# The first activations of a fused convolution and gated feed-forward kernel: loaded as fp32 in four pieces by SyncE and ScalarE, cast by ScalarE

## The chip, the cores and the metric

The kernel runs on one core of a Trainium2 chip. The metric is the device time of one execution in microseconds, as the median of several runs. Five engines of the core take part: TensorE (PE), VectorE (DVE), ScalarE (ACT), GpSimd (POOL) and SyncE (SP). SP, ScalarE and GpSimd can issue DMA transfers; a transfer that also converts fp32 to fp16 on its way is issued by GpSimd in this kernel.

## The reference

There are two steps. A lightweight causal convolution over `x` (8 x 4096 x 192, fp32): each of 8 heads covers 24 of the 192 channels and has 7 taps, which are a softmax over `weight` (8 x 7). Then a gated feed-forward of width 1536 over all 32768 tokens:

```python
w = softmax(weight)                                   # per head, 7 taps
conv[b, s, h, :] = sum_k w[h, k] * x_pad[b, s + k, h, :]   # 6 zeros ahead of each sequence
t = conv.reshape(32768, 192)
out = (np.maximum(t @ w_gate, 0) * (t @ w_val)) @ w_out    # 192 -> 1536 -> 192
```

## The kernel before

The eight sequences are handled as two streams (`st` 0 and 1: sequence b and b + 4) of which 1024 tokens each make a unit; there are 16 units (`NUNIT`). A unit's convolved activations lie transposed in `xc[u]` (64 channels of each of the two streams on 128 partitions, three channel blocks `c`, 1024 tokens). `gate_val` multiplies them with `Wg` and `Wv` (line 505, matmuls 512 wide), ScalarE applies the ReLU (line 516), VectorE multiplies (line 517), and `project` multiplies with `Wo` (lines 536, 556, 594). The convolution of units 2 to 15 is done with per-channel multiplications on VectorE, ScalarE and GpSimd beside the matmuls of earlier units; units 0 and 1 are convolved on TensorE with band matrices.

The order of work on each engine is the order of the program (`manual_schedule`); waits come from the data. The start, which the change touches, goes as follows.

- **The first x.** The first window is 512 tokens of both streams, in `xts[0]`, cut into five blocks `jj` of 104 tokens with 6 tokens of history. Blocks 1 to 4 of stream 0 are loaded by SP as fp32 (line 125) into a staging place in the room of the tile `prods`, which is not needed until later, and are cast by ScalarE in one instruction (line 279). Blocks 1 to 4 of stream 1 are loaded by GpSimd straight into fp16 (line 130). Block 0 of both streams is loaded by SP as fp32 (line 141) behind rows that VectorE has set to zero (line 140) and cast by VectorE (line 294).
- **The taps and the bands.** SP loads `weight` (line 104); VectorE takes the maximum (line 214), ScalarE the exponential (line 217), ahead of which its table load (line 148) and a first, unused exponential stand; VectorE the sum, its reciprocal and the scaled head selection `over` (lines 221 to 224). GpSimd makes a mask (`affine_select`, line 131) for it. TensorE spreads the taps (lines 235 and 255) into two PSUM tiles, and these are copied into band matrices: heads 0 to 2 and head 3 by VectorE, heads 4 to 7 by ScalarE (line 288, `fill_band`). Short matmuls on constants (line 157, `warm_up`) stand in TensorE's gaps.
- **The first window.** `conv_dense(0, c)` for `c` = 0, 1, 2 multiplies the blocks with the bands (line 333). For `c` = 0 the order is blocks 1 to 4 of stream 0, blocks 1 to 4 of stream 1, then block 0 of both. Channel block 0 takes heads 0 to 2, block 1 heads 2 to 5, block 2 heads 5 to 7. ScalarE copies channel blocks 0 and 2 to `xc[0]`, VectorE block 1 (line 343). Then the first `gate_val` begins.
- **Weights.** GpSimd loads `Wg` and `Wv` in six cuts of columns with a cast (line 173, `load_w`) to partitions 0 to 63. The other 64 partitions are copied on the core: cuts 0 and 1 by VectorE (`both_halves`), the others by GpSimd (`pool_halves`, line 180). Between the weights GpSimd loads the second window's x (`load_x(1)`, line 90), and after them what the later units need.

Of the kernel before, what the change touches and what calls it, by code (L numbers as in the profile page):

```python
# [9 lines left out]
F16 = mybir.dt.float16  # L10
# [5 lines left out]
def kernel(  # L16
# [12 lines left out]
    nc = tc.nc  # L29

    B, S, D = x.shape
    H, KW = weight.shape
    G = D // H
    DFF = moe_w_gate.shape[1]
    PAD = KW - 1
    NB = B // 2
    NCH = D // 64
    NBLK = D // 32
    NFF = DFF // 128
    WIN = 512  # L40
    NWIN = S // WIN
    SUB = 112
# [4 lines left out]
    GSUB = 5  # L47
    DSUB = 104
# [13 lines left out]
    const = ctx.enter_context(tc.tile_pool(name="const", bufs=1))  # L62
# [35 lines left out]
    xts = {}  # L98
    ROWS0 = DSUB + PAD
# [7 lines left out]
    def stage(p0, rows, st, n_st, jj, n):  # L107
        at = room[p0 : p0 + rows, 0, 0, 0:1]
        dims = [[D * GSUB, n_st], [D, n], [1, D]]
        return bass.AP(  # L110
            tensor=at.tensor,
            offset=at.offset + D * (GSUB * st + jj),
            ap=[at.ap[0]] + [d for d in dims if d[1] > 1],
        )

    xts[0] = xpool.tile([128, GSUB, 2, D], F16, name="x_h")

    def body(st):
        return bass.AP(
            tensor=x.tensor,  # L120
            offset=x.offset + (NB * st * S + DSUB - PAD) * D,
            ap=[[D, SUB], [DSUB * D, GSUB - 1], [1, D]],
        )

    nc.sync.dma_start(out=stage(0, SUB, 0, 1, 1, GSUB - 1), in_=body(0))
    ones = const.tile([128, SUB], FP)
    nc.vector.memset(ones[:], 1.0)
    spaced = const.tile([SUB, KW, SEG + 2 * GAP], FP)
    nc.gpsimd.memset(spaced[:], 0.0)  # L129
    nc.gpsimd.dma_start(out=xts[0][0:SUB, 1:GSUB, 1, :], in_=body(1))  # L130
    nc.gpsimd.affine_select(
        out=spaced[:, :, GAP : GAP + SEG],
        in_=ones[0:SUB, 0 : KW * SEG].rearrange("p (k s) -> p k s", k=KW),
# [8 lines left out]
        out=stage(PAD, DSUB, 0, 2, 0, 1),  # L142
        in_=bass.AP(
            tensor=x.tensor, offset=x.offset, ap=[[D, DSUB], [NB * S * D, 2], [1, D]]
        ),
    )
    spare = const.tile([H, 1], FP)
    nc.scalar.activation(spare[:], ones[0:H, 0:1], ACTF.Exp)

# [12 lines left out]

    Wg = const.tile([128, NCH, DFF], F16)
    Wv = const.tile([128, NCH, DFF], F16)
    Wo = const.tile([128, NFF, D], F16)
    CUTS = [0, 128, 384, 640, 896, 1152, DFF]

    def load_w(s, to=None):  # L170
        cols = slice(CUTS[s], CUTS[to or s + 1])
        for src, dst in ((moe_w_gate, Wg), (moe_w_val, Wv)):
            nc.gpsimd.dma_start(
                out=dst[0:64, :, cols],
                in_=src.rearrange("(c p) f -> p c f", p=64)[:, :, cols],
            )

    def both_halves(copy, s, dst):
        cols = slice(CUTS[s], CUTS[s + 1])
        copy(out=dst[64:128, :, cols], in_=dst[0:64, :, cols])  # L180

    def pool_halves(s):
        both_halves(nc.gpsimd.tensor_copy, s, Wg)
        both_halves(nc.gpsimd.tensor_copy, s, Wv)

    load_w(0)
    load_w(1)
    load_w(2)
    xts[1] = load_x(1)
    load_w(3)  # L190
    pool_halves(2)
    load_w(4, 6)
    pool_halves(3)

    ex = const.tile([H, KW + 1, SEG], FP)
# [3 lines left out]
    def summed(out, step, n, at):  # L199
# [15 lines left out]
        out=mx[:], in_=wr[:], axis=mybir.AxisListType.X, op=ALU.max, negate=True  # L215
# [9 lines left out]
        out=over[:],  # L225
# [10 lines left out]
        out=spread[0:SUB, 0, 0:H],  # L236
# [7 lines left out]
    with nc.allow_low_precision("products with one and zero"):  # L244
        nc.vector.tensor_tensor(
            out=diag[:],
# [6 lines left out]
    for a in range(2):  # L253
        for b in range(NSEG):
            nc.tensor.matmul(
                out=(bps, spread)[a][:, a, HB * SEG * b : HB * SEG * (b + 1)],
# [12 lines left out]
    for h in range(H):  # L269
        r = G * h  # L270
        while r < G * (h + 1):
            c, n = r // 64, min(64 - r % 64, G * (h + 1) - r)
            nc.sync.dma_start(
                out=tap[r % 64 : r % 64 + n, c, :],
                in_=taps[h : h + 1, :].unsqueeze(1).to_broadcast([1, n, KW]),
            )
            r += n

    nc.scalar.copy(out=xts[0][0:ROWS0, 1:GSUB, 0, :], in_=stage(0, ROWS0, 0, 1, 1, GSUB - 1))
    bands = {}  # L280

    def fill_band(a, heads, copy):
        lo, n = heads[0] - HB * a, len(heads)
        part = const.tile([128, n, SUB], F16, name=f"band{heads[0]}")
        for i, h in enumerate(heads):
            bands[h] = part[0 : SUB + PAD, i, :]
        from_ = (bps, spread)[a][:, a, 0 : HB * SUB]
        copy(
            out=part[:].rearrange("p h (b s) -> p h b s", s=SEG),
            in_=from_.rearrange("p (b h s) -> p h b s", h=HB, s=SEG)[:, lo : lo + n],  # L290
        )

    fill_band(0, [0, 1, 2], nc.vector.tensor_copy)
    nc.vector.tensor_copy(out=xts[0][0:ROWS0, 0, :, :], in_=stage(0, ROWS0, 0, 2, 0, 1))
    fill_band(0, [3], nc.vector.tensor_copy)
    fill_band(1, [4, 5, 6, 7], nc.scalar.copy)

# [10 lines left out]
    def conv_dense(g, c):  # L308
# [3 lines left out]
        if g == 0 and c == 0:  # L312
            xc[0] = xcpool.tile([128, NCH, UNIT], F16, name="xc")
            both_halves(nc.vector.tensor_copy, 0, Wg)
            both_halves(nc.vector.tensor_copy, 0, Wv)
# [324 lines left out]
    both_halves(nc.vector.tensor_copy, 1, Wg)  # L640
    both_halves(nc.vector.tensor_copy, 1, Wv)
    pool_halves(4)
    pool_halves(5)
    nc.gpsimd.tensor_copy(out=tap[64:128], in_=tap[0:64])
# [71 lines left out]
```

## Time and profile before

| | |
|---|---|
| Median of 3 runs | 767.79 us (767.7 to 768.71) |
| Profiled execution, its own time | 767.88 us |
| Span in its profile | 765.9 us |
| TensorE busy | 761.7 us (99%) |
| VectorE, ScalarE, GpSimd busy | 692.7, 600.7, 369.9 us |
| First matmul of line 505 | 7.80 us after the start of the span |

Times in the views are microseconds from the start of the span unless marked ns. A line of the timeline gives start, duration, engine, line of the kernel, operation, the tiles written and read with their shapes, and in brackets the engine's idle time just before with what ended it. In the chain of work that ended last, each piece is what the next one waited for. In the DMA view, q1 is SP's queue and q0 GpSimd's, with packets, megabytes written and the time of the packets as a share of the 16 DMA engines; it can be above 100%, since packets overlap on an engine. TensorE's matmuls are pipelined, so its busy share is not a share of its peak.

### The profile page before, as it was taken

How to read it: one execution, taken by the hardware profiler on the slowest of the kernel's cores; microseconds unless marked ns; L12 is line 12 of the kernel's file. 1: busy time of each engine (PE TensorE's matmuls, PEld its weight loads, DVE VectorE, ACT ScalarE, POOL GpSimd, SP SyncE). 2: the span in 40 equal slices, each digit the busy share in tenths (PEclk: the TensorE clock that was granted, in tenths of full speed). 3: DMA queues.
4: the chain of work that ended last, by engine and by line, in shares of the span. 5: the costliest groups of instructions: out<-in, count | busy, mean ns of one | idle time of the engine just before them, and what ended most of it. 6: DMA issues, size and time to landing. Idle time of an engine off the chain costs nothing.

```text
span 765.9 us, 24782 instructions
## 1 busy us (share of the span) xinstructions
PE 761.7 (99%) x10794; PEld 502.5 (66%) x10794; DVE 692.7 (90%) x746; ACT 600.7 (78%) x735; POOL 369.9 (48%) x212
## 2 busy tenths in 40 slices
PE   9999999999999999999999999999999999999998
PEld 4595674946749476584755848567484674947648
DVE  7999999999999999999999999999999999996591
ACT  6797887878878787887878878788787887875571
POOL 8608648093570926619166290743908346090000
PEclk9999999999999999999999999999999999999999
DMA  8966727190472804528054281722919131200202
GB/s 121 134 104 116 92 91 88 54 122 6 100 78 66 110 23 97 61 85 95 23 111 47 85 92 44 106 31 85 93 44 117 21 92 39 65 22 15 71 2 84
DMA packets 131810, 56.12 MB, mean 73 GB/s; under 512 B 96741, under 2 KB 131701, under 8 KB 131701
## 3 DMA queue, kind: packets, MB, share of 16 engines
q1 hardware_dynamic: 90789, 38.85, 25.1%
q0 software_dynamic: 40768, 15.59, 18.9%
q8 instruction: 84, 1.38, 0.8%
q14 instruction: 25, 0.20, 0.1%
q10 hardware_dynamic: 144, 0.10, 0.0%
HBM read 31.68 MB, written 25.17 MB: 74 GB/s over the span
## 4 chain that ended last, share of the span: by engine, by line
PE 99%; DMA 1%; issue 0%; POOL 0%; ACT 0%; POOLq 0%
PE ps L505 65%; PE ps L536 31%; PE ps L556 2%; DMA x_h<-in_x_dram 1%; PE ps L594 1%; PE ps L333 0%; PE ps L358 0%; POOL spaced L129 0%; ACT acc L573 0%; POOLq L700 0%
## 5 line engine op out<-in xcount | busy, mean ns | idle before, releaser
L517 DVE TENSOR_TENSOR hT<-gr,ps 128x1024 f16<-128x1024 f16 (+1 forms) x386 | 468.9, 1215 | 37.0 <-ACT gr L516 9.9
L516 ACT ACTIVATE gr<-ps 128x1024 f16<-128x1024 f32 (+1 forms) x386 | 392.9, 1019 | 102.4 <-PE ps L505 100.6
L458 POOL TENSOR_TENSOR prods<-prods 128x1344 f32<-128x1344 f32 x70 | 212.4, 3034 | 309.1 <-DVE prods L454 305.7
L505 PE MATMUL ps<-xc,Wg 64*128 64x512 f16 x2304 | 311.9, 376 | 0.0
L505 PE MATMUL ps<-xc,Wv 64*128 64x512 f16 x2304 | 311.8, 376 | 0.0
L536 PEld LDWEIGHTS <-hT 64*128 64x128 f16 x5664 | 234.1, 94 | 3.6
L536 PE MATMUL ps<-Wo,hT 64*128 64x192 f16 x5664 | 236.1, 243 | 0.0
L505 PEld LDWEIGHTS <-Wv 64*128 64x128 f16 x2304 | 129.8, 94 | 118.5 <-DVE hT L517 0.3
L505 PEld LDWEIGHTS <-Wg 64*128 64x128 f16 x2304 | 112.2, 94 | 132.4 <-issue 0.2
L481 DVE SCALAR_TENSOR_TENSOR acc<-x_r,tap,acc 128x576 f32<-128x576 f16 x210 | 154.3, 811 | 1.6 <-ACT acc L469 1.6
L452 ACT ACTIVATE prods<-x_r,tap 128x448 f32<-128x448 f16 x222 | 130.3, 662 | 0.0
L573 ACT COPY out_s<-ps 128x768 f32<-128x768 f32 (+1 forms) x63 | 45.7, 725 | 52.4 <-PE ps L536 42.5
L414 POOL DMA_DIRECT2D x_e<-in_x_dram x56 | 45.1, 818 | 3.4 <-POOL x_p L433 3.4
L433 POOL COPY x_p<-x_e 128x1728 f16<-128x1728 f16 x28 | 44.7, 1624 | 1.7 <-DMA x_e<-in_x_dram 1.6
L458 POOL TENSOR_TENSOR xc<-prods 128x1344 f16<-128x1344 f32 x14 | 42.4, 3027 | 1.1
L481 DVE SCALAR_TENSOR_TENSOR xc<-x_r,tap,acc 128x576 f16<-128x576 f16 x42 | 31.8, 810 | 0.0
L573 DVE COPY out_s<-ps 128x384 f32<-128x384 f32 x15 | 8.3, 550 | 25.5 <-ACT out_s L573 25.5
L469 ACT ACTIVATE acc<-x_r,tap 128x576 f32<-128x576 f16 x42 | 29.4, 766 | 0.0
L454 DVE TENSOR_SCALAR prods<-x_r,tap 128x448 f32<-128x448 f16 x72 | 27.3, 446 | 0.0
L556 PE MATMUL ps<-Wo,hT 128*128 128x192 f16 x192 | 16.2, 246 | 0.0
L556 PEld LDWEIGHTS <-hT 128*128 128x128 f16 x192 | 15.9, 98 | 0.0
L90 POOL DMA_DIRECT2D x_h<-in_x_dram x6 | 4.9, 825 | 0.0
(54 smaller groups left out, 66.9 us busy)
## 6 DMA issues: line engine op xcount, KB each, us to landing
out_dram<-out_s SPq DMA_DIRECT2D x63, 384.0 KB
x_e<-in_x_dram POOLq DMA_DIRECT2D x34, 192.0 KB, 6.2
x_e<-in_x_dram POOLq DMA_DIRECT2D x22, 240.0 KB, 4.8
x_r<-x_p SPq DMA_TRANSPOSE x126
Wo<-in_moe_w_out_dram POOLq DMA_DIRECT2D x1, 576.0 KB
x_h<-in_x_dram POOLq DMA_DIRECT2D x2, 240.0 KB, 7.6
x_h<-in_x_dram POOLq DMA_DIRECT2D x2, 210.0 KB, 5.1
x_h<-in_x_dram POOLq DMA_DIRECT2D x2, 192.0 KB, 7.6
```

The source lines that it names most:

```text
L414: nc.gpsimd.dma_start(out=xe[:, j : j + n, st, :, :].rearrange("p j c r -> p j (c r)"), in_=bass.AP(tensor=x.tensor, offset=x.offset + (b ...
L433: nc.gpsimd.tensor_copy(out=xp[:, :, :, st, :], in_=xe[:, :, st, :, :])
L452: engine.activation(out=out, in_=in_, func=ACTF.Copy, scale=scale)
L458: nc.gpsimd.tensor_tensor(out=pr[:, 0] if k < KW - 1 else xc[u][:, :, LDVE:UNIT], in0=pr[:, 0], in1=pr[:, k], op=ALU.add,)
L469: nc.scalar.activation(out=accs[u][:, c, :], in_=shifted(u, c, 0, 0), func=ACTF.Copy, scale=tap[:, c, 0:1],)
L481: nc.vector.scalar_tensor_tensor(out=xc[u][:, c, 0:LDVE] if k == KW - 1 else acc[:, c, :], in0=shifted(u, c, k, 0), scalar=tap[:, c, k : k ...
L505: nc.tensor.matmul(out=pss[i][:, st, :], lhsT=W[64 * st : 64 * st + 64, c, 128 * f : 128 * (f + 1)], rhs=xcb[64 * st : 64 * st + 64, c, WI ...
L516: nc.scalar.activation(out=gr[:, sts], in_=pss[0][:, sts], func=ACTF.Relu)
L517: nc.vector.tensor_tensor(out=h[:, f, sts], in0=gr[:, sts], in1=pss[1][:, sts], op=ALU.mult)
L536: mm = nc.tensor.matmul(out=outs[q], lhsT=h[64 * r : 64 * r + 64, f, st, 128 * q : 128 * (q + 1)], rhs=Wo[64 * r : 64 * r + 64, f, :], sta ...
L556: nc.tensor.matmul(out=outs[q], lhsT=h[:, f, st, 128 * q : 128 * (q + 1)], rhs=Wo[:, f, :], start=(f == 0), stop=(f == NFF - 1),)
L573: one(out=dst[:, step * j : step * j + step], in_=src[:, step * j : step * j + step])
```

## The change

All of the first x now comes as fp32 through the staging place. Blocks 1 and 2 of stream 0 are issued by ScalarE as its first instruction, blocks 3 and 4 by SP, then block 0 of both streams as before, then blocks 1 and 2 and blocks 3 and 4 of stream 1, also by SP. ScalarE casts these four pieces, each 384 columns wide, in that order, ahead of its band of heads 4 to 7. GpSimd no longer loads the first x: its first transfer is the first cut of `Wg`, ahead of the mask; the first cut of `Wv` and the rest follow as before. On VectorE the cast of block 0 goes ahead of the bands of heads 0 to 2 instead of behind them. The definitions of the weight tiles and helpers move up; only `load_w` gets a new argument.

```diff
-    def body(st):
+    def body(st, jj, n):
         return bass.AP(
             tensor=x.tensor,
-            offset=x.offset + (NB * st * S + DSUB - PAD) * D,
-            ap=[[D, SUB], [DSUB * D, GSUB - 1], [1, D]],
+            offset=x.offset + (NB * st * S + DSUB * jj - PAD) * D,
+            ap=[[D, SUB], [DSUB * D, n], [1, D]],
         )
 
-    nc.sync.dma_start(out=stage(0, SUB, 0, 1, 1, GSUB - 1), in_=body(0))
+    nc.scalar.dma_start(out=stage(0, SUB, 0, 1, 1, 2), in_=body(0, 1, 2))
+    nc.sync.dma_start(out=stage(0, SUB, 0, 1, 3, 2), in_=body(0, 3, 2))
     ones = const.tile([128, SUB], FP)
     nc.vector.memset(ones[:], 1.0)
     spaced = const.tile([SUB, KW, SEG + 2 * GAP], FP)
     nc.gpsimd.memset(spaced[:], 0.0)
-    nc.gpsimd.dma_start(out=xts[0][0:SUB, 1:GSUB, 1, :], in_=body(1))
...
+    def load_w(s, to=None, which=(0, 1)):
+        cols = slice(CUTS[s], CUTS[to or s + 1])
+        for src, dst in [((moe_w_gate, Wg), (moe_w_val, Wv))[i] for i in which]:
...
+    load_w(0, 1, (0,))
     nc.gpsimd.affine_select(
...
             tensor=x.tensor, offset=x.offset, ap=[[D, DSUB], [NB * S * D, 2], [1, D]]
         ),
     )
+    for jj in (1, 3):
+        nc.sync.dma_start(out=stage(0, SUB, 1, 1, jj, 2), in_=body(1, jj, 2))
     spare = const.tile([H, 1], FP)
     nc.scalar.activation(spare[:], ones[0:H, 0:1], ACTF.Exp)
...
-    load_w(0)
+    load_w(0, 1, (1,))
     load_w(1)
     load_w(2)
     xts[1] = load_x(1)
...
-    nc.scalar.copy(out=xts[0][0:ROWS0, 1:GSUB, 0, :], in_=stage(0, ROWS0, 0, 1, 1, GSUB - 1))
+    for st in range(2):
+        for jj in (1, 3):
+            nc.scalar.copy(
+                out=xts[0][0:ROWS0, jj : jj + 2, st, :], in_=stage(0, ROWS0, st, 1, jj, 2)
+            )
...
+    nc.vector.tensor_copy(out=xts[0][0:ROWS0, 0, :, :], in_=stage(0, ROWS0, 0, 2, 0, 1))
     fill_band(0, [0, 1, 2], nc.vector.tensor_copy)
-    nc.vector.tensor_copy(out=xts[0][0:ROWS0, 0, :, :], in_=stage(0, ROWS0, 0, 2, 0, 1))
     fill_band(0, [3], nc.vector.tensor_copy)
     fill_band(1, [4, 5, 6, 7], nc.scalar.copy)
```

More of the change, by code (lines that the diff above doesn't have):

```diff
@@ L129, with both_halves, pool_halves @@
     nc.gpsimd.memset(spaced[:], 0.0)
-    nc.gpsimd.dma_start(out=xts[0][0:SUB, 1:GSUB, 1, :], in_=body(1))
+    Wg = const.tile([128, NCH, DFF], F16)
+    Wv = const.tile([128, NCH, DFF], F16)
+    Wo = const.tile([128, NFF, D], F16)
+    CUTS = [0, 128, 384, 640, 896, 1152, DFF]
+    def load_w(s, to=None, which=(0, 1)):
+        cols = slice(CUTS[s], CUTS[to or s + 1])
+        for src, dst in [((moe_w_gate, Wg), (moe_w_val, Wv))[i] for i in which]:
+            nc.gpsimd.dma_start(
+                out=dst[0:64, :, cols],
+                in_=src.rearrange("(c p) f -> p c f", p=64)[:, :, cols],
+            )
+    def both_halves(copy, s, dst):
+        cols = slice(CUTS[s], CUTS[s + 1])
+        copy(out=dst[64:128, :, cols], in_=dst[0:64, :, cols])
+    def pool_halves(s):
+        both_halves(nc.gpsimd.tensor_copy, s, Wg)
+        both_halves(nc.gpsimd.tensor_copy, s, Wv)
+    load_w(0, 1, (0,))
     nc.gpsimd.affine_select(
@@ L161 @@
     warm_up(512, 512, 512, 512, 512, 512, 128)
[L165 to L184, printed above, removed]
-    load_w(0)
+    load_w(0, 1, (1,))
     load_w(1)
@@ L277 @@
             r += n
-    nc.scalar.copy(out=xts[0][0:ROWS0, 1:GSUB, 0, :], in_=stage(0, ROWS0, 0, 1, 1, GSUB - 1))
+    for st in range(2):
+        for jj in (1, 3):
+            nc.scalar.copy(
+                out=xts[0][0:ROWS0, jj : jj + 2, st, :], in_=stage(0, ROWS0, st, 1, jj, 2)
+            )
     bands = {}
```

## The prediction

> **What bounds the kernel now.** I read the page first, its chain of work that ended last:
>
> ```profile
> PE 99%; DMA 1%; issue 0%; POOL 0%; ACT 0%; POOLq 0%
> ```
>
> TensorE carries 99% of the way to the end. The change touches nothing but the first microseconds, so I took the same chain in order of time:
>
> ```profile
> 1.43 4.86 DMA x_h<-in_x_dram
> 6.29 0.04 issue
> 6.33 1.53 PE ps L333 x104
> 7.87 6.61 PE ps L505 x60
> ```
>
> From 7.87 us on the chain is TensorE alone, to 762.81 us. What stands ahead of it is one transfer: the second stream's four blocks of the first x, which GpSimd issues with a cast at 1.43 us and which TensorE sees at 6.29 us. Whatever moves the first matmul of L505 moves the end by as much; nothing else in the edit can. The timeline gives the places and durations (start, us, engine, line):
>
> ```profile
> 1.29 0.34 SPq L125 DMA_DIRECT2D prods<-in_x_dram  x1
> 1.43 0.88 POOL L130 DMA_DIRECT2D x_h<-in_x_dram  x1 [0.28 <-issue]
> 2.38 0.39 ACT L217 ACTIVATE ex<-wr,mx 8x112 f32<-8x112 f32 x1
> 2.67 0.68 POOL L173 DMA_DIRECT2D Wg<-in_moe_w_gate_dram  x1
> 4.83 0.83 ACT L279 CAST x_h<-prods 110x768 f16<-110x768 f32 x1 [1.30 <-DMA prods<-in_x_dram]
> 5.11 0.51 DVE L288 CAST band<-ps 128x336 f16<-128x336 f32 x1 [0.62 <-PE ps L255]
> 5.55 0.45 DVE L294 CAST x_h<-prods 110x384 f16<-110x384 f32 x1
> 5.57 0.53 ACT L288 CAST band<-ps 128x448 f16<-128x448 f32 x1
> 7.00 0.58 ACT L343 CAST xc<-ps 128x512 f16<-128x512 f32 x1 [0.91 <-PE ps L333]
> 7.46 0.69 DVE L343 CAST xc<-ps 128x512 f16<-128x512 f32 x1
> 7.80 0.39 PE L505 MATMUL ps<-xc,Wg 64*128 64x512 f16 x2
> 8.24 0.38 PE L505 MATMUL ps<-xc,Wg 64*128 64x512 f16 x2
> 763.18 0.37 ACTq L574 DMA_DIRECT2D out_dram<-acc  x1
> ```
>
> The second stream becomes usable 0.29 us after the last band (5.57 + 0.53 = 6.10, and DVE's at 6.18). The DMA view of the stretches 3 to 4, 4 to 5 and 5 to 6.3 us shows what the transfers do meanwhile (queue: packets, MB, share of 16 engines; q1 is SP's, q0 GpSimd's):
>
> ```profile
> q1 hardware_dynamic: 467, 0.35, 103.7%
> ...
> q0 software_dynamic: 287, 0.11, 92.0%
> q1 hardware_dynamic: 168, 0.12, 46.4%
> ...
> q0 software_dynamic: 689, 0.21, 158.0%
> ```
>
> The DMA engines are full from 3.0 us: 467 packets of 768 bytes in a microsecond from SP alone, 287 + 168 = 455 from two queues together, 530 per us from GpSimd alone. About 500 packets per us is the limit, whoever issues. Two lags follow. SP's first piece has 448 packets; 50 had moved by 3.0 us and 467 per us after, so it was complete at 3.9 us, and ScalarE saw it at 4.83: 0.95 us. GpSimd's 448 were complete at 5 + (448 - 291)/530 = 5.3 us and TensorE saw them at 6.29: 0.99 us. Take 0.97 from moved to seen.
>
> **Part by part.** *GpSimd* loses one issue of 0.88 us. Its first weight piece goes at 1.43 (0.68 us), the mask follows at about 2.2 (it was at 2.38, and its first reader on VectorE is at 3.26), and the later weight and x issues come up to 0.9 us earlier. TensorE waits for none of them today (the first weights' copies on VectorE end at 7.34, before the first converted block at 7.58), so this gains nothing by itself; its price is that weight packets now run beside x instead of behind it.
>
> *ScalarE* gets a DMA issue ahead of its table load. Nearest row: its own issue at the end, 0.37 us; SP's take 0.34 to 0.46. Table load, the two exponentials and the taps come later by that; `ex` starts at about 2.70 instead of 2.38, since ScalarE was free at 2.31 and had 0.07 us to spare. Behind `ex` queue VectorE's sums, TensorE's spreading matmuls and the bands: bands 0 to 2 start at 5.4 instead of 5.11. The moved cast of block 0 (0.45 us) fits ahead of them into VectorE's idle 0.62 us plus this delay if its data is there by 4.95; packets 449 to 656 move near 4.0, seen near 4.95, so between 0 and 0.45 us more. Either way those bands end at 6.0 to 6.4, still ahead of the last x piece below: cost nothing, 0.3 if that cover went.
>
> *The x transfers.* x is now 448 + 208 + 448 = 1104 packets, all on hardware queues. ScalarE's piece starts at 0.83 instead of 1.29, so I let the full rate begin 0.46 us earlier, at 2.54 (bounds: 1.8 us, when the tiny `weight` load moves its packets, and 3.0 as now). By 3.9 us that gives 1.36 x 470 = 640 packets. GpSimd's first packet came 2.5 us after its issue began (1.43 to just under 4.0), so the first weight piece (192 packets) arrives at 3.9 again and takes its part: by 4.6 us x has 640 + 350 - 192 = 798, by 5.0 us 986, and the last 118 go beside the next 192 weight packets at about 300 per us: complete at 5.4. Seen at 5.4 + 0.97 = 6.37. Without any weights it would be 2.54 + 1104/470 = 4.9 and 5.86.
>
> [...]
>
> *The casts.* ScalarE's one cast of 768 columns (0.83 us) becomes four of 384. Half of 0.83 is 0.42, and 448 columns took 0.53: I take 0.46, plus 0.04 to start TensorE as in the chain. Three run while the fourth's data is on its way; the fourth is bare. TensorE gets the last piece at 6.37 + 0.46 + 0.04 = 6.87 instead of 6.33: **0.54 later**. Fewer matmuls are left behind it, 16 of channel block 0 instead of 24, at 1.53/104 = 15 ns: **0.12 earlier**. The band of heads 4 to 7 (0.53 us) is queued on ScalarE behind the fourth cast, so it ends at 7.38 instead of 6.10. Channel block 1 needs it and would else start 16 x 15 ns after 6.87, at 7.1 and a little: **0.28 later** for blocks 1 and 2. Block 1's copy has 0.09 us to spare today (7.46 + 0.69 = 8.15 against its first matmul at 8.24), but VectorE's weight copies are no longer beside it; call that nothing. Block 0's copy on ScalarE begins when its matmuls are done, just after that band: no cost.
>
> The sum is 0.54 - 0.12 + 0.28 = **0.7 us later**. The profiled execution took 767.88 us (span 765.9 and 1.98 around it), 0.09 above the median of 767.79. So 768.58 by its own time, **768.5** against the median. That is 0.09%: I count up to 0.2%, 1.54 us, as no change, about what a measurement of this kernel can tell; the three times shown themselves span 1.0 us.
>
> **The rivals.**
> 1. *The start comes earlier* (chance 0.17). The slow stretch from 2.2 to 3.0 us (50 packets) is a first-touch cost that ScalarE's early piece takes for all, and the full rate begins near 1.9 us. Then x is complete at 1.9 + 2.35 = 4.25, with one weight piece beside it 4.4, seen at 5.4, cast by 5.9: 0.43 earlier than 6.33. Bands, at 6.0 to 6.4, then limit: about 0.3 us earlier, 767.5; at best 0.8. For it: ScalarE does nothing before 0.82. Against: nothing shows what the slow stretch is.
> 2. *Slower: no head start, and weights take turns with x* (0.17). ScalarE's issue stands behind its table load (0.82 to 2.10), or its queue needs as long to warm up as SP's. Then x has 470 packets at 3.9, 628 at 4.6, 816 at 5.0; the other 288 share with unbroken weight traffic, at the 57 packets per quarter microsecond that SP's queue had beside GpSimd's between 4.25 and 4.5 us, 228 per us: complete at 6.3, at TensorE at 7.8. That is 1.47 - 0.12 + 0.28 = 1.6 us later, 769.4. It decides once x is complete after 6.2 us.
> 3. *The array's clock* (0.03). At the start a 512 wide L157 matmul follows the other every 0.43 us, at 7.8 us every 0.22: the array runs at half its pace until about 5 us. Should the longer wait bring that back for as long as it lasted (0.86 to 5.1 us), 4.3 us of L505 would cost twice their time: 2.1 us, 769.9. The granted clock in the windows is 1.00 throughout and the forecast wait is under 0.6 us, so I hold it unlikely. [...]
>
> **How the numbers follow.** The forecast, 0 to 1.4 us later, has 0.63. Rival 1 lies within 0.2% but for 0.03 (an execution that gains more than worked out); rival 2 has 0.12 of its 0.17 above 1.54 us; rival 3 is above. With 0.03 for more than I see on the slow side: slower 0.12 + 0.03 + 0.03 = 0.18, faster 0.03, same 0.79. The range goes from 767.3 (rival 1 with a little scatter) to 769.7 (rival 2 with a little more sharing); the forecast's own is 767.8 to 769.2.
>
> **What would show it.** After: the chain should lead through ScalarE's last cast instead of the GpSimd transfer; that cast should end near 6.8, L288 of ScalarE near 7.4, the first L505 near 8.3, and L505 to L594 take as long as now. ScalarE's DMA issue should stand ahead of the table load at 0.82. A last cast before 6.2 means rival 1, after 7.6 rival 2; 512 wide pairs of L505 at 0.43 us behind 8 us mean rival 3. I am wrong altogether if TensorE shows waits after 20 us that it has not now.

## The result and the profile after

The changed kernel takes 772.29 us (median of 5 runs, 771.92 to 773.17) against 768.18 us of five runs of the kernel before: 1.0051 times as long, 95% interval 1.004 to 1.0062. It is 4.1 us slower, outside the predicted range. The profiled execution took 772.29 us with a span of 770.3, 4.4 us more than before.

The page's chain of work that ended last, of the changed kernel, has new members beside TensorE:

```profile
PE 99%; DMA 1%; ACT 0%; DVE 0%; SPq 0%; issue 0%
```

In order of time (start, us, what; L340 is the old L333, L512 the old L505):

```profile
2.14 5.29 DMA prods<-in_x_dram
...
7.46 0.52 ACT x_h L284
...
7.99 3.24 PE ps L340 x113
11.23 7.43 PE ps L512 x60
```

From the end of that last piece on, at 18.66 us, the chain takes 748.3 us, as it did before from 14.48 us on. All of the loss lies in the first 19 us. The timeline of the changed kernel shows where:

```profile
1.37 0.81 POOL L139 DMA_DIRECT2D Wg<-in_moe_w_gate_dram  x1 [0.21 <-issue]
2.66 0.37 ACT L220 ACTIVATE ex<-wr,mx 8x112 f32<-8x112 f32 x1
5.59 0.72 PE L181 MATMUL ps<-const-bfloat16-1.0 128*128 128x512 bf16 x2
6.82 0.71 DVE L300 CAST x_h<-prods 110x384 f16<-110x384 f32 x1 [2.00 <-DMA prods<-in_x_dram]
8.27 0.51 ACT L284 CAST x_h<-prods 110x384 f16<-110x384 f32 x1 [0.30 <-DMA prods<-in_x_dram]
8.83 2.16 PEld L340 LDWEIGHTS <-x_h 110*32 110x32 f16 x96 [0.20 <-ACT x_h L284]
11.17 0.61 PE L512 MATMUL ps<-xc,Wg 64*128 64x512 f16 x2
11.57 0.64 PE L512 MATMUL ps<-xc,Wv 64*128 64x512 f16 x2
12.85 0.39 PE L512 MATMUL ps<-xc,Wg 64*128 64x512 f16 x2
13.07 0.38 PE L512 MATMUL ps<-xc,Wv 64*128 64x512 f16 x2
```

Two things are to be seen. The last piece of x is cast at 8.27 and reaches TensorE at 8.83 us, where the second stream was usable at 6.33 before: **2.50 us**. And TensorE is slow: its first pairs of L512 start 0.40 to 0.43 us apart, and only from 12.85 us on 0.22 apart as before. From the last piece to the end of the 60 matmuls it takes 18.66 - 8.83 = 9.83 us, before 14.48 - 6.33 = 8.15: **1.68 us**. Together 4.18 us, the shift of the whole chain; the other 0.2 us of the span lie behind the last matmul.

The DMA view of the stretches 3 to 4, 4 to 5 and 5 to 6 us, to be held against 467, 168 + 287 and 689 packets before (the last in 1.3 us):

```profile
q1 hardware_dynamic: 179, 0.13, 67.5%
q0 software_dynamic: 48, 0.01, 12.2%
...
q1 hardware_dynamic: 187, 0.14, 55.1%
q0 software_dynamic: 92, 0.02, 30.7%
...
q1 hardware_dynamic: 324, 0.23, 77.9%
q0 software_dynamic: 164, 0.05, 44.1%
```

Between 3 and 5 us the DMA engines are not full: 80% and 86% with both queues added, where the kernel before has 105% and 138%, and they move 227 and 279 packets. A packet of SP's queue also takes longer, 60 ns (67.5% of 16 us over 179 packets) against 36 ns before (103.7% over 467). So there x is held back by something else than a full machine. From 5 us on the engines are full (122% with both queues), and x shares them with GpSimd's loads: from 6.25 to 7 us SP's queue moves 33, 20 and 22 packets per quarter microsecond beside GpSimd's 71, 82 and 84. The last packet of x moves at 7.32 us.

In the experiments such counts are given per quarter microsecond, and "seen" is when the cast of a piece starts. SP's counts include packets of 4 bytes, 13 or 16 at the end of each transfer of x, up to 14 in a quarter microsecond, so that 131 can stand for 118 of x.

### The profile page after: what moved, and what is told of

The parts are those of the page before. It is cut to its first block, busy times and chain, and to the rows that moved or that the text cites. A ratio compares the mean times of both kernels' runs of the same rounds, so it can differ in the third digit from the quotient of the medians.

```text
span 770.3 us, 24787 instructions
## 1 busy us (share of the span) xinstructions
PE 764.1 (99%) x10794; PEld 504.5 (65%) x10794; DVE 693.4 (90%) x746; ACT 601.6 (78%) x738; POOL 369.3 (48%) x211
## 4 chain that ended last, share of the span: by engine, by line
PE 99%; DMA 1%; ACT 0%; DVE 0%; SPq 0%; issue 0%
PE ps L512 65%; PE ps L543 30%; PE ps L563 2%; DMA prods<-in_x_dram 1%; PE ps L340 1%; PE ps L601 1%; PE ps L365 0%; ACT x_h L284 0%; DVE prods L162 0%; SPq L163 0%; ACT acc L580 0%; DVE ones L128 0%; DVE ex L199 0%; DVE places L175 0%
## 5 line engine op out<-in xcount | busy, mean ns | idle before, releaser
L512 PE MATMUL ps<-xc,Wg 64*128 64x512 f16 x2304 | 312.5, 377 | 0.0
L512 PE MATMUL ps<-xc,Wv 64*128 64x512 f16 x2304 | 312.4, 377 | 0.0
L512 PEld LDWEIGHTS <-Wv 64*128 64x128 f16 x2304 | 130.4, 94 | 118.6 <-issue 0.8
L512 PEld LDWEIGHTS <-Wg 64*128 64x128 f16 x2304 | 112.3, 94 | 132.5 <-issue 0.9
L340 PE MATMUL ps<-band,x_h 110*32 110x104 f16 (+7 forms) x240 | 5.1, 248 | 1.7 <-ACT x_h L284 1.7
```

What stands on the lines that cost most here:

```text
L512: nc.tensor.matmul(out=pss[i][:, st, :], lhsT=W[64 * st : 64 * st + 64, c, 128 * f : 128 * (f + 1)], rhs=xcb[64 * st : 64 * st + 64, c, WI ...
```

## The experiments

The theories for the transfers: A, the early weights slow x down; B, several transfers in a row on SP's queue are slow by themselves; C, first reads of a place in x are slow; D, small pieces; E, something else at that time, such as SP's loads of the taps; F, rows 12.6 MB apart. For TensorE: too little work ahead of the convolution leaves the array at a slow pace. "Later weights" below always means the edit of the first run. Where one time is given without an interval, the run was a single execution, and times of packets and casts come from one profiled execution each.

**Weights later** (`e1_weights_later`).

```diff
-    load_w(0, 1, (0,))
+    nc.gpsimd.memset(room[:, 5, 0:2, :], 0.0)
...
-    load_w(0, 1, (1,))
+    load_w(0)
```

> The changed kernel, but GpSimd writes 0.9 us of zeros into an unused part of the staging room where the first piece of Wg stood, and issues both first weight pieces behind the mask, about when the kernel before did (2.7 us instead of 1.4). Theory A (weight transfers issued early slow the x transfers down): x moves at some 470 packets per us to its end, block 0 is seen by VectorE by 5.0 us instead of 6.82, the last piece by ScalarE by 6.0 instead of 8.27, and the kernel is within 1.2 us of before. Theory B (four transfers in a row on SP's queue are slow by themselves, whatever GpSimd does): block 0 still at 6.3 or later, the last piece at 7.8 or later, the time still 3.5 us or more above before. Theory C (the second stream's part of x is slow at its first touch): as B, with the slow stretch where block 0 starts.

Measured: 772.03 us, ratio 1.0048 (1.0033 to 1.0063), no faster. Block 0 is cast at 5.85 instead of 6.82, the last piece at 7.46 instead of 8.27. A explains 0.8 us of the arrival, but the slow stretch stays: with no GpSimd packet before 4.5 us, SP's queue moves 61, 63 and 46 packets per quarter microsecond between 3.25 and 4.0. The weights are later but not gone: from 4.75 us on GpSimd's queue moves 27, 58 and 64 packets per quarter beside x, and no run here has x without them to its end. What was won was lost on TensorE. The chain in order of time:

```profile
8.03 2.40 PE ps L340 x71
10.42 8.52 PE ps L512 x60
```

The last piece comes 0.8 us earlier than in the changed kernel, and the 60 matmuls end at 18.94 instead of 18.66 us. The granted clock of this run shows the array losing its pace (stretch, its length, busy time of PE, PEld, DVE, ACT and POOL, then the granted clock, DMA share and GB/s):

```profile
4.07:7.48 3.41, 2.05 (x43) 1.47 (x43) 1.67 (x5) 1.07 (x4) 3.41 (x6) 1.00 1.19 192
7.48:14.31 6.83, 6.34 (x120) 3.66 (x118) 3.39 (x7) 3.18 (x6) 4.47 (x7) 0.50 1.30 156
```

**Bands first on VectorE** (`e2_bands_first`).

```diff
-    nc.vector.tensor_copy(out=xts[0][0:ROWS0, 0, :, :], in_=stage(0, ROWS0, 0, 2, 0, 1))
     fill_band(0, [0, 1, 2], nc.vector.tensor_copy)
+    nc.vector.tensor_copy(out=xts[0][0:ROWS0, 0, :, :], in_=stage(0, ROWS0, 0, 2, 0, 1))
```

> The changed kernel with VectorE's cast of block 0 put back behind the bands of heads 0 to 2. The transfers should not move, so the last x piece still comes at 8.3. If the order on VectorE costs nothing of its own (last piece and clock decide): within 0.4 us of the changed kernel. If it is what lets TensorE idle and so keeps the array slow: bands at 5.5 and first convolution matmuls at 6.1 instead of 7.99, the array at full pace for L512 (pairs every 0.22 us) and 1.0 to 1.7 us less than the changed kernel.

Measured: 772.38 us, 1.0052 (1.0037 to 1.0067). The bands come at 5.44 and TensorE starts at 6.24, but it waits again for x, and pairs of L512 are 0.43 us apart until 12.9 us. The order on VectorE costs nothing of its own.

**More warm-up matmuls** (`e3_more_warm`).

```diff
-    warm_up(512, 128)
+    warm_up(512, 128, 512, 512, 512, 512)
```

> The changed kernel with four more 512 wide warm-up matmuls behind the last two, which fill TensorE's idle time from 6.3 to 8.0 us. If the array is slow because TensorE had too little to do before the convolution: the convolution behind the last piece takes 1.5 us instead of 2.4, the pairs of L512 come every 0.22 us from the first on, and the kernel is 1.2 to 1.7 us faster than the changed one, some 2.5 us slower than before. If the slow pace is not caused by idling: no difference to the changed kernel within 0.4 us.

Measured: 770.69 us, 1.0033 (1.0019 to 1.0048), by the medians 1.6 us less than the changed kernel; the two intervals overlap, and one of the six times, 772.82 us, is as slow as the changed kernel. The four matmuls ran by 6.5 us, not up to 8.0, because the array already had its pace at 4.3 us in the profiled execution (771.62 us). The chain in order of time:

```profile
9.02 0.52 ACT x_h L284
...
9.58 1.51 PE ps L340 x94
11.10 6.87 PE ps L512 x60
```

The last piece comes even later in this execution (9.02), but the convolution takes 1.51 us for 94 matmuls and pairs of L512 are 0.22 us apart from the first. From the last piece to the end of the 60 matmuls it takes 8.38 us, against 9.83.

**ScalarE's piece alone, in the kernel before** (`e4_act_piece_only`).

```diff
-    nc.sync.dma_start(out=stage(0, SUB, 0, 1, 1, GSUB - 1), in_=body(0))
+    nc.scalar.dma_start(out=stage(0, SUB, 0, 1, 1, 2), in_=body(0, 1, 2))
+    nc.sync.dma_start(out=stage(0, SUB, 0, 1, 3, 2), in_=body(0, 3, 2))
```

> The kernel before with one part of the change alone: blocks 1 and 2 of stream 0 issued by ScalarE, blocks 3 and 4 by SP; all else as before, the second stream by GpSimd with its cast. If the head start is harmless: the taps and bands 0.3 us later, the first stream's data 0.5 us earlier, the second stream at 6.0 to 6.4 and the time within 0.4 us of before. If the 0.3 us later taps alone leave the array at its slow pace: pairs of L505 every 0.43 us at first and 1.2 to 2 us slower than before.

Measured: 769.1 us, 1.0009 (1.0 to 1.0018). The first stream is there at 4.03 instead of 4.83, the bands at 5.35; but block 0, whose cast found its data waiting at 5.55 before, is waited for until 6.41, and the convolution runs at the slow pace (120 matmuls in 3.51 us). SP's queue moves 37, 34 and 11 packets per quarter from 3.25 us on: the slow stretch comes with this part alone. Of ten runs two took 767.7 and 767.8, the others 768.4 to 769.3.

**The second stream from rows that were read before**, with later weights (`e5_later_same_rows`) and with early ones (`e6_same_rows`).

```diff
-            offset=x.offset + (NB * st * S + DSUB * jj - PAD) * D,
+            offset=x.offset + (DSUB * jj - PAD) * D,
...
-            tensor=x.tensor, offset=x.offset, ap=[[D, DSUB], [NB * S * D, 2], [1, D]]
+            tensor=x.tensor, offset=x.offset, ap=[[D, DSUB], [0, 2], [1, D]]
```

> The run with the later weights, but all loads of the second stream's first window (block 0 and the four others) read the rows of the first stream, which have been read already; it computes the second stream's first window from the wrong rows. Theory C (rows of a part of x that nothing has read yet come slowly at first): the stretch from 3.25 to 4.0 us goes at 100 packets or more per quarter microsecond instead of 61, 63 and 46, block 0 is seen by 5.0 instead of 5.85 and the last piece by 6.2 instead of 7.46. Theory D (more and smaller transfers on the hardware queues are slow, whatever they read) and theory E (something else at that time): 5.7 to 6.0 and 7.2 to 7.7, as there.

> The changed kernel with the same replacement of the second stream's rows and the weights as early as it has them. Theory C for x alone: block 0 by 5.2 instead of 6.82, last piece by 6.5 instead of 8.27. If the early weights do the rest (they too are first reads): block 0 gains 0.5 to 1.0 us, the last piece as much, and both stay over 0.7 us behind the run with the later weights and the same rows. Theories D and E: 6.5 to 7.1 and 7.9 to 8.6.

Measured: block 0 at 5.46 and the last piece at 6.91 with later weights, 6.49 and 7.97 with early ones. The stretch from 3.25 to 4.0 stays (46, 63, 48 and 23, 29, 35), so C fails there; behind it the pieces go faster. The weights' place is worth 1.0 us, as A has it. The first run is at 769.13 us beside 768.27 of before, with the array at full pace; the second at 771.82 without it.

**Reading places of the second stream ahead**, by SP (`e7_touch`) and by GpSimd (`e9_gpsimd_touch`, with later weights).

```diff
+    nc.sync.dma_start(
+        out=room[0:16, 5, 0, 0:40].rearrange("p (j d) -> p j d", d=8),
+        in_=bass.AP(
+            tensor=x.tensor, offset=x.offset + NB * S * D, ap=[[7 * D, 16], [DSUB * D, 5], [1, 8]]
+        ),
+    )
     nc.scalar.dma_start(out=stage(0, SUB, 0, 1, 1, 2), in_=body(0, 1, 2))
```

> The changed kernel with one small load more on SP, ahead of its pieces of x: 8 numbers of 80 rows of the second stream, five for each of 16 partitions, spread over its first window, into an unused place. It costs SP 0.35 us. Theory C: the slow stretch is over by the time block 0 comes, which is seen 0.5 to 1.2 us earlier than 6.82, the last piece by 7.5 instead of 8.27. Theories D and E: both as late as in the changed kernel or 0.3 us later.

> The run with the later weights, where GpSimd, instead of writing 0.9 us of zeros, issues two small loads of 8 numbers of 80 rows each, one for each stream, spread over its first window in five places for each of 16 partitions, into an unused place. Theory C, sharpened (a DMA engine's first reads in each far place of x are slow, some two to five packets per engine, and the rest is fast; the loads at full rate before hide them): the stretch from 3.25 to 4.0 us moves 90 packets or more per quarter microsecond instead of 61, 63 and 46, block 0 is seen by 5.2 instead of 5.85 and the last piece by 6.8 instead of 7.46. Without it: within 0.3 us of 5.85 and 7.46, or later by what the small loads take.

Measured: with SP's small load block 0 comes at 5.92, but the stretch has only moved: now SP's first piece of x has it (33, 21, 41, 48 from 3.0 us on) and is cast at 5.31, and the last piece comes at 8.17; 772.08 us. It is the third transfer again, counting ScalarE's and the small one, and not block 0. GpSimd's loads moved their first packets at 3.25 us, too late to be ahead of anything; 5.83 and 7.50 (769.91 us, with the array at full pace) decide nothing.

**Long pieces on SP** (`e8_big_pieces`: later weights, bands first, no load on ScalarE).

```diff
-    nc.scalar.dma_start(out=stage(0, SUB, 0, 1, 1, 2), in_=body(0, 1, 2))
-    nc.sync.dma_start(out=stage(0, SUB, 0, 1, 3, 2), in_=body(0, 3, 2))
+    nc.sync.dma_start(out=stage(0, SUB, 0, 1, 1, 4), in_=body(0, 1, 4))
...
-    for jj in (1, 3):
-        nc.sync.dma_start(out=stage(0, SUB, 1, 1, jj, 2), in_=body(1, jj, 2))
+    nc.sync.dma_start(out=stage(0, SUB, 1, 1, 1, 4), in_=body(1, 1, 4))
```

> The changed kernel with later weights, the bands ahead of block 0 on VectorE, no load on ScalarE, and each stream's blocks 1 to 4 as one transfer of SP (448 packets each, block 0 between them): the second stream as fp32 by SP, else like before. Theory D (small pieces): full rate from 3.0 on, 470 packets per us, block 0 seen by 5.6, the second stream complete at 5.4 and cast from 6.4. Theory C: full rate from 3.0 to 3.9, then the slow stretch when block 0 begins, the second stream's cast not before 7.0.

Measured: 770.35 us beside 768.27. 97 to 131 packets per quarter from 3.0 to 4.0 us, no stretch with idle engines afterwards, but 66 to 89 with full ones; block 0 at 5.67, the whole second stream at 7.11. Three transfers in a row on SP do not make the stretch, so B falls as it was put; but behind the first 448 packets the rate drops here as well. Neither D nor C alone.

**Taps later** (`e10_taps_later`) moves the taps' ScalarE step and their SP loads behind the first window; **near rows** (`e11_near_rows`) replaces `NB * st * S` by `WIN * st`, for block 0 too. Both with later weights.

> The run with the later weights, with the taps' last ScalarE step and their ten loads on SP (issued from 3.8 to 11.1 us, each 0.5 to 0.9 us of SP) moved behind the convolution of the first window. Theory E (SP's issuing of those loads holds up the transfers queued ahead of them): from 4.25 us on x moves at 100 packets or more per quarter microsecond instead of 65 to 77, the last piece is seen by 6.9 instead of 7.46. Without it: 7.2 to 7.6, and block 0 at 5.7 to 5.9 in either case.

> The run with the later weights, with the second stream's first window read 512 tokens further in the first sequence instead of four sequences away (12.6 MB); it computes the second stream's first window from the wrong rows. Theory F (rows that lie 12.6 MB apart, read in turn by block 0, get in each other's way): no slow stretch at 3.25, block 0 by 5.2, last piece by 6.7. Theory C: those rows have not been read either, so block 0 at 5.6 to 5.9 and the last piece at 7.1 to 7.6.

Measured: block 0 at 5.97 and the last piece at 7.93 without the taps' loads, 6.21 and 7.82 with near rows, all later than 5.85 and 7.46 (771.28 and 772.36 us). E's taps and F fall. How far such times scatter can be seen from the changed kernel, the run with bands first and the one with more warm-up, which have the same transfers: last cast at 8.27, 8.36 and 9.02.

**GpSimd's x first, in the kernel before** (`e12_gpsimd_x_first`).

```diff
+    nc.gpsimd.dma_start(out=xts[0][0:SUB, 1:GSUB, 1, :], in_=body(1))
     nc.sync.dma_start(out=stage(0, SUB, 0, 1, 1, GSUB - 1), in_=body(0))
...
-    nc.gpsimd.dma_start(out=xts[0][0:SUB, 1:GSUB, 1, :], in_=body(1))
```

> The kernel before with one move: GpSimd issues the second stream's load as its first instruction, ahead of zeroing the mask's tile, so at 0.8 instead of 1.43 us. If the second stream's arrival bounds the start and its queue keeps its pace: usable by TensorE at 5.7 to 6.0 instead of 6.29, then the band of heads 4 to 7 bounds (6.1), first L505 0.1 to 0.3 us earlier, a difference that the comparison cannot tell from none. If it collides with SP's pieces instead: the first stream later than 4.83 and the start later by as much.

Measured: 768.33 us, 1.0002 (0.9993 to 1.0011). GpSimd issues at 1.39, not at 0.8: this order gains nothing, and no version here beats the kernel before.

**Everything read before** (`e13_all_read_before`), **block 0 last** (`e14_block0_last`), **two long transfers, one on each queue** (`e15_scalar_stream1`) and **all pieces on SP** (`e16_sp_all_pieces`), all with later weights. The first is `e5_later_same_rows` with block 0 read from `x.offset + DSUB * D`; the second swaps SP's issues; the others are

```diff
+    nc.scalar.dma_start(out=stage(0, SUB, 1, 1, 1, 4), in_=body(1, 1, 4))     # e15
+    nc.sync.dma_start(out=stage(0, SUB, 0, 1, 1, 4), in_=body(0, 1, 4))       # e15
...
+    nc.sync.dma_start(out=stage(0, SUB, 0, 1, 1, 2), in_=body(0, 1, 2))       # e16
     nc.sync.dma_start(out=stage(0, SUB, 0, 1, 3, 2), in_=body(0, 3, 2))       # e16
```

> The run with the later weights; block 0 of both streams and all of the second stream's first window are read from rows of the first stream that the two first pieces have read already (wrong rows). Theory C (first reads of a place): no slow stretch, 90 packets or more per quarter microsecond from 3.25 us on, block 0 seen by 5.0 and the last piece by 6.3. If the stretch stays (60 or fewer from 3.25 to 4.0, block 0 after 5.4), first reads are not its cause.

> The run with the later weights, with block 0 last on SP's queue, behind the second stream's pieces (and VectorE's bands of heads 0 to 2 ahead of its cast). If block 0's own transfer is slow (13 engines, two places 12.6 MB apart): the second stream's first piece moves at 100 or more per quarter microsecond from 3.25, is seen by 4.8 and its second by 5.4, block 0 by 6.5. If the stall comes at that time whatever stands there (C, or the end of ScalarE's transfer): the first piece not before 5.5, the second not before 6.0, block 0 after 6.5.

> Another division of the same work: ScalarE issues the second stream's blocks 1 to 4 in one transfer at 0.83 us, SP the first stream's in one at 1.29 and block 0 behind it; weights later and bands first as in the runs before. If short pieces on a queue are what stalls: two queues full to the end, all of x complete by 4.9 us and seen by 5.9, the last cast by 6.8, a time within 0.6 us of before. If the limit is any fp32 load of this size by the hardware queues after some 450 packets: the last piece seen after 6.5, and 1 us or more above before.

> The run with the later weights and the bands first on VectorE, with the first piece also issued by SP (ahead of its others) instead of ScalarE. If ScalarE's transfer ahead is the cause of the stall: 110 packets or more per quarter microsecond from 3.0 to 4.0 us, as in the kernel before and with the long transfers on SP (97 to 131), and 65 to 90 after that. If short pieces are: a stretch of 60 or fewer for three quarter microseconds somewhere between 3.25 and 4.75.

Measured. With every row read before, the stretch is there all the same and the pieces behind it run at full rate. The DMA view of this run, 3.25 to 3.5 and 4.5 to 4.75 us:

```profile
q1 hardware_dynamic: 39, 0.03, 71.8%
...
q1 hardware_dynamic: 107, 0.08, 101.0%
```

Block 0 is seen at 5.23, the last piece at 6.70; 768.86 us beside 767.83. With block 0 last, the second stream's first piece has the stretch (35, 53, 44, 54) and is seen at 5.93, the second at 6.79, block 0 at 7.95 (771.86 us): it is not block 0's own. With five pieces on SP the stretch comes too, at the third of them (68, 43, 39, 55 from 3.5 us on), and the last piece is seen at 8.10 (772.46 us beside 767.9): ScalarE's transfer ahead is not its cause. The same view, 4.0 to 4.25 us, first of this run, then of the one with long pieces on SP:

```profile
q1 hardware_dynamic: 39, 0.03, 58.4%
```

```profile
q1 hardware_dynamic: 89, 0.07, 113.7%
```

With one long transfer on each queue (770.09 us, 1.0029, 1.0017 to 1.004) the engines stay full (110% to 115% from 3.75 to 5.0 us at 65 to 92 packets per quarter), but the queues hardly take turns: SP's, issued 0.46 us after ScalarE's, has moved one packet of x by 3.25 us, when ScalarE's (q10) runs at full rate. The stretches 3.0 to 3.25 and 4.0 to 4.25 us:

```profile
q10 hardware_dynamic: 121, 0.09, 107.5%
q1 hardware_dynamic: 1, 0.00, 0.9%
...
q1 hardware_dynamic: 65, 0.05, 112.0%
```

Of the two expectations the second came: block 0, the last, is seen at 6.96, and the run is 2.3 us above before. Here ScalarE's packets are the second stream's, and they come at full rate; SP's are the first stream's, and they come slowly. So it is not the second stream's place in x that is slow, but what is queued behind the first 448 packets.

**Less warm-up in the kernel before** (`e17_less_warm`).

```diff
-    warm_up(512)
...
-    warm_up(512, 128)
```

> The kernel before without the three warm-up matmuls behind the taps' spreading (one 512 wide, then 512 and 128); nothing else moves, TensorE does less between 4.1 and 5.6 us. If such idling alone leaves the array at its slow pace: the convolution from 6.33 on takes 2.4 us or more for its 104 matmuls instead of 1.53, pairs of L505 come every 0.43 us for some microseconds, and the kernel is 1.2 to 2 us slower. If not: within 0.3 us of before.

Measured: 769.39 us, 1.0017 (1.0006 to 1.0027); single runs from 767.74 to 770.65. The loads are issued as before (first stream cast at 4.86). The chain in order of time of the profiled execution has TensorE slow at first:

```profile
5.74 3.13 PE ps L331 x83
8.88 6.72 PE ps L503 x60
```

The first L503 starts at 8.81 instead of 7.80. Less work for TensorE alone, with no transfer changed, costs this.

## Why the prediction was wrong

The frame held in the main: the start alone decides, and nothing new waits after 19 us. But "whatever moves the first matmul of L505 moves the end by as much" did not hold: that matmul came 3.37 us later (11.17 against 7.80) and the chain's end 4.2 us, because the array was slow beyond it. ScalarE's issue stood ahead of its table load and the full rate began at 2.3 to 2.5 us, as forecast; `ex` came at 2.66 (forecast 2.70), so the head start was there. Two terms failed.

**The rate of the x transfers.** The step "about 500 packets per us is the limit, whoever issues" was read from one long transfer of SP and from GpSimd's queue (where only 164 of the 689 packets were x's; 479 were the weights', of 256 and 512 bytes), and the sum let five short pieces run at that rate. The forecast had x complete at 5.4 and TensorE served at 6.87; it was 8.83, **1.96 us** more. The last cast's time can be divided so, as an estimate: 5.86 by the sum without weights; 6.70 measured with later weights and all rows read before, so at most 0.8 us for the slow stretch, which the sum did not have (the last packets share the engines with weights from 5.1 us on in this run too); 7.46 with later weights and the proper rows, 0.8 us for rows read for the first time (0.5 in the run that left block 0 to new rows), which it did not have either; 8.27 as changed, 0.8 us for the early weights (1.0 with rows read before), for which it had 0.5. The weights' first packet moved at 3.25 us, not at 3.9 as the sum had it. These are single executions, and the scatter seen above is as large as each part. What they show is that the stretch comes at the third of several short pieces, whichever piece it is, whichever queue issues the first, and whatever rows it reads, that the engines are partly idle in it, and that long pieces do not have it. Long pieces are not free of the wrong step either: in both runs that have them, what is queued behind the first 448 packets comes at 65 to 92 packets per quarter with full engines, while rows that had been read came at 97 to 113 behind the stretch. Why, stays open in both cases.

Rival 2 had the right place, x complete after 6.2 us, and half of its condition: weights did run beside x, but it needed the head start to be missing too. By its price the arrival alone comes to 2.50 - 0.12 + 0.28, some 2.7 us. What the arrival cost with the array at full pace is in the run with more warm-up, whose median is 2.8 us over the 767.9 beside it.

**The array's pace.** Rival 3 had a chance of 0.03, and its sign came: 1.68 us from the last piece to the end of the 60 matmuls, where the sum had 0.28 - 0.12 = 0.16, so **1.52 us** more. Its price was about right (2.1 us were named), its chance was not, for two reasons. The granted clock was cited against it and reads 1.00 in the changed kernel too, while pairs of L512 stand 0.43 us apart. But that trace holds no granted clock before 12.86 us, which is where the pace changes, and a stretch without one reads 1.00 (so from 11.0 to 11.5 us, where the pairs stand 0.40 us apart). The kernel before holds none before 5.03 us, so the 1.00 that the prediction read at the start said nothing. Where a trace has a record, clock and pace agree, as with later weights above.

And its mechanism, the pace lost in the wait, is not what the changed kernel's trace shows: there the array never had it. The warm-up pair at 5.59 us takes 0.72 us where the kernel before takes 0.44. Four other runs do show a pace that is there and is lost around the wait: with later weights, long pieces on SP, taps later and all pieces on SP the granted clock is 1.00 from 3.5 to 4.7 us on and falls to 0.50 between 6.95 and 8.13 us (with all pieces on SP a 512 wide matmul takes 0.39 us at 3.90, as at full pace, but eight matmuls of the convolution take 0.53 us at 7.86, against 0.36 with more warm-up). So there are two ways to a slow array, and rival 3 named one.

The 0.3 us by which the taps came later, costed "nothing", opened gaps in TensorE's work ahead of the convolution. That they decide is not shown. Of the 14 profiled executions with the later taps, eight had no full pace before 9.4 us and six had it by 4.8; the four with taps about as before and all warm-up matmuls had it by 5.1. The same program up to that point falls in both groups: with more warm-up a 512 wide matmul takes 0.39 us at 4.3 us, in the changed kernel 0.61. By the medians, filling the wait gains 1.6 us and taking work out of the kernel before loses 1.5 us; only the second has an interval that is clear of its comparison.

Between two changes of the granted clock lie 3.41 or 6.83 us at the start (with later weights it is 1.00 from 4.07 to 7.48 us and 0.50 from there to 14.31), and the first record stands at 4.07 us in that execution, at 4.72 or 12.86 in others. What sets these places is not shown; as the same program falls in both groups, chance has a part in which group an execution falls into. One long idle stretch is not what took the pace away: with later weights the clock fell at 7.48 us, TensorE was busy for 2.05 us of the 3.41 before that, and it never waited longer than 1.3 us. With GpSimd's small loads it was busy for 2.09 us of a stretch as long (from 4.1 us on) and kept its pace, so what decides is open.

The rest of the sum was close. From the last piece to the end of the 60 matmuls the forecast is 8.15 + 0.16 = 8.31 us; the runs at full pace took 8.38 (more warm-up), 8.18 (same rows) and 8.43 (GpSimd's small loads). The order on VectorE cost nothing, as forecast, though its cover was thinner than thought: the bands waited for block 0 until 7.45.

## What to carry to other kernels

The transfer rate read from one long transfer (467 packets in a microsecond) did not hold here for the same bytes in short pieces (39 to 68 in a quarter microsecond, with all pieces on SP): before a load is cut up or moved to another queue, find a row of the trace with that size and queue, and set the range by its absence. Nor did it hold for a second long transfer behind the first (66 to 89, with long pieces on SP). Where TensorE waits at the start, price the pace of the array as its own term and read it from the start-to-start times of equal matmuls (0.43 against 0.22 us here), and try filler matmuls where the change opens a gap (1.6 us by the medians here, with intervals that overlap). Before a granted clock of 1.00 is taken as full pace, see where the trace's clock records begin (5.03 and 12.86 us here). The weights that came early, for which nobody waited yet, cost the last cast of x 0.8 us here (8.27 against 7.46, single executions): such loads belong behind those that somebody waits for.

## What the hardware showed

- Short fp32 pieces of 208 to 224 packets on the hardware queues ran into a stretch of some 1 us with engines partly idle (39 to 68 packets per quarter microsecond with all five on SP, against 100 ahead of it); pieces of 448 did not, but behind the first of them the rate fell to 65 to 92 with full engines.
- GpSimd's converting load moved the same second stream at up to 120 packets per quarter microsecond (4.75 to 5.0 us, kernel before), SP's fp32 load in one long piece behind others at 66 to 89 (long pieces on SP), ScalarE's, with nothing ahead of it, at 121 to 122 (one long transfer on each queue).
- With one long transfer on each queue two hardware queues were served nearly one after the other: 121 packets of ScalarE's against 1 of SP's from 3.0 to 3.25 us, some 2 us after SP's issue. Whether SP's queue had nothing to move by then or was not served, the runs do not tell.
- GpSimd's first packet came 1.9 us after the issue began as changed (1.37 to 3.25) and 2.5 us before (1.43 to 3.94), ScalarE's and SP's about 1 us after theirs when no load of x was ahead (0.83 to 1.91 as changed, 1.29 to 2.29 before; 1.7 to 2.0 us for SP's with ScalarE's long one ahead).
- With later weights the granted clock of TensorE was 1.00 for 3.41 us and 0.50 for the next 6.83, and it fell after a stretch in which TensorE was busy for 60% of the time (2.05 of 3.41 us).
